# One product of a pair's first unit moved behind the second unit, with the gathering and the sums of pieces in another order

## The chip, the cores and the metric

The kernel runs on one core of one Trainium2 chip. The metric is the device time of one execution in microseconds (us). Five engines work side by side, each through its own instructions in order: PE (matrix products), DVE and ACT (elementwise work), POOL and SP, which here mostly send transfers (DMAs). They wait for one another through semaphores. Sums of products are built in PSUM, which has eight banks; everything else lies in SBUF or in device memory.

## The reference

Let `xn` be x (2048 rows of 448) after a layer norm. The result is x + s * silu(g), with

```
a = xn @ dft_hid_re.T ;  b = xn @ dft_hid_im.T
s = dft_seq_re @ a - dft_seq_im @ b          # 2048 x 2048 matrices
g = (gelu(xn @ w_gate) * (xn @ w_up)) @ w_down
```

The change concerns s alone, in the last stage, from about 491 us on.

## The kernel before, in words

Operands that need more than one pass are held as a high half (rounded, type fp32r) and a low half (the rest). ACT writes the high half and DVE subtracts it to get the low half; the helper `split` does both, at lines L119 (ACT) and L120 (DVE).

The first stages compute the norm, then g by products of gate, up and down, and then a and b for all 16 tiles of 128 rows of the sequence. During the stage of g, sums of matrices of C (the sequence matrices) are made by transfers and kept in device memory (`sums`). silu(g) goes to device memory too (`gv`).

**The last stage.** The rows of the result (index t) are treated in eight pairs of row tiles, j = 0 to 7. For each pair the kernel runs 16 steps, called units, numbered u = 0 to 15 within the pair and m through all pairs. Units 0 to 13 (`u < NS`, NS = 14) each take one sequence tile k and use a scheme of seven products in place of eight: the seven pieces of C for this pair and tile, each 128 x 128, are multiplied with seven pieces of a and b, called T (`TS[k]`, each piece 224 columns in high and low halves, so 448 wide). Each product has its own PSUM bank and sums up over the 14 units. In `seven` (L971) one product is two matmuls: the high half of the C piece by the whole T piece (L977), and the low half by the high half of T (L980). Units 14 and 15 ("t0", "t1") add the two sequence tiles left over by plain products, unit 14 for the first row tile and unit 15 for the second (`plain`, L992 to L994), each in a bank `py`.

**Banks.** Seven products and one plain product make eight banks; unit 15 uses the bank of the first product again. From pair to pair the list of banks turns by one, so that the last of the seven products of the next pair takes the bank in which unit 14 of this pair left its plain product. That product starts only when DVE has read the bank, at L1074.

**Pieces of C.** `load_c` (L870) loads a unit's raw pieces: three from `ct` (L881) and two from `sums` (L882), by SP; for units 14 and 15 one load from `cp` (L879). `sum_c` (L884) forms two more pieces on DVE (L888, L889, 128 x 128 each). `prep_c` (L893) splits all pieces of a unit into high and low halves, in one of four buffers that go round with m, and then loads the raw pieces of the unit five later into the place just freed. At step m the main loop calls `sum_c(m + 4)` and then `prep_c(m + 3)`.

**End of a pair.** `gather` (L996) takes the seven sums out of their banks into the four quarters of the pair's result, two row tiles `cc`: ACT copies the first product (L1000), then seven additions on DVE follow (L1002 to L1008). Three of these run at step 13, the other four at step 14; L1074 adds the plain product of unit 14 at step 15. What is left is put in the list `spare`, of which one entry is taken per step from step 0 of the next pair: for the first row tile add the two halves (L1021) and multiply with silu(g) (L1015) and have POOL add x by an accumulating transfer (L1017); add the second plain product (L1096); the same two for the second row tile. The two finished row tiles are stored by SP (L1019) at steps 5 and 8 (`STORE_AT`).

**Swaps.** Not all T tiles fit into SBUF. Two of them are replaced in each pair, in eight transfers by SP (L1045) at steps 2 to 9. In the last pair, step 12 runs units 12 and 13 together, product by product, and the gathering takes place there.

The order on each engine is the order in which this program calls the operations. There is no planner; only waits for data, for free buffers and for free banks delay an instruction.

Of the kernel before, what the change touches and what calls it, by code (L numbers as in the profile page):

```python
# [13 lines left out]
P = 128  # L14
S = 2048
D = 448
DX = 512
F = 1792
NK = S // P
# [8 lines left out]
HD = D // 2  # L28
# [6 lines left out]
NS = len(KS)  # L35


def order(j):

    return [*KX[j % 2], *KR, *KX[(j + 1) % 2]]  # L40
# [5 lines left out]
def fnet_geglu(ctx: ExitStack, tc: tile.TileContext, x, ca, ct, cp, et, wgu, wd, out):  # L46
# [13 lines left out]
    nc = tc.nc  # L60
# [37 lines left out]
    def bank(i, name):  # L98
        return psum.tile([P, 512], F32, name=name, tag=f"b{i}")
# [18 lines left out]
    def split(h, l, src):  # L118
        nc.scalar.activation(h, src, AF.Copy)  # L119
        nc.vector.tensor_sub(l, src, h)  # L120
# [300 lines left out]
    with tc.manual_schedule():  # L421
# [366 lines left out]
        TS, ab, behind = {}, {}, []  # L788
# [61 lines left out]
        units = [(j, k) for j in range(NK // 2) for k in order(j) + ["t0", "t1"]]  # L850
        UN = NS + 2

        def raw_at(m):
            if m in (4, 5, 9, 10):
                return cc[:, 896 * ((m + 1) % 5) :][:, :896]
            i = (2, 0, 1, 2, 0, 0, 0, 1, 2)[m] if m < 9 else (m - 11) % 5
            return a_r[:, 896 * i :][:, :896] if i < 3 else new["d0"][:, 896 * (i - 3) :][:, :896]
# [4 lines left out]
        def slot_at(m):  # L862
            return (
                lambda: (rest(new["tmp"]), rest(a_x[0])),
                lambda: (unit_at(0), unit_at(1)),
                lambda: (unit_at(2), unit_at(3)),
                lambda: (unit_at(4), rest(a_x[3])),
            )[m % 4]()
# [15 lines left out]
        def sum_c(m):  # L884

            if m < len(units) and not isinstance(units[m][1], str):
                _, cr1, ci1, s2, s1, _, s4 = [raw_at(m)[:, i * P : (i + 1) * P] for i in range(7)]
                nc.vector.tensor_add(s2, cr1, s1)  # L888
                nc.vector.tensor_add(s4, s2, ci1)  # L889

        c_hl = {}

        def prep_c(m):  # L893

            if m >= len(units):
                return
            n = (4 if isinstance(units[m][1], str) else 7) * P
            h, l = [v[:, :n] for v in slot_at(m)]
            split(h, l, raw_at(m)[:, :n])
            c_hl[m] = h, l  # L900
            n = nxt.get(m, m + 5)
            if n:
                load_c(n)

        for k in [*range(14), 15, 14]:
            ps = hid_mm(k)
# [52 lines left out]
        def load_gx(j, t):  # L959
            if 2 * j + t < NK:  # L960
                nc.sync.dma_start(gx[t], gv[:, 2 * j + t])


        LOAD_AT = 2
        STORE_AT = 5, 8
        GX_AT = 11, 12

        PARTS = slice(0, 6, 5), slice(2, 4), slice(4, 7, 2), slice(1, 2)
        PRODUCTS = {1: (1, 0), 6: (3, 5), 2: (2, 2), 7: (5, 3), 5: (4, 4), 3: (6, 6), 4: (0, 1)}

        def seven(m, ps, n=1):  # L971

            for q, (i, b) in PRODUCTS.items():
                for u in range(m, m + n):
                    v = TS[units[u][1]][:, b * D : (b + 1) * D]
                    h, l = [w[:, i * P : (i + 1) * P] for w in c_hl[u]]
                    nc.tensor.matmul(  # L977
                        ps[q][:, :D], h, v, start=u % UN == 0, stop=False, skip_group_check=True
                    )
                    nc.tensor.matmul(  # L980
                        ps[q][:, :HD], l, v[:, :HD],
                        start=False, stop=u % UN == NS - 1, skip_group_check=True,
                    )

        def plain(m, py):
            h, l = c_hl.pop(m)
# [9 lines left out]
        def gather(ps):  # L996

            p = {q: v[:, :D].rearrange("p (w d) -> p w d", w=2) for q, v in ps.items()}
            c11, c12, c21, c22 = [cv[t][:, :, s] for t in range(2) for s in range(2)]
            nc.scalar.activation(c11, p[1], AF.Copy)  # L1000
            return [
                lambda: nc.vector.tensor_sub(c12, c11, p[6]),  # L1002
                lambda: nc.vector.tensor_add(c11, c11, p[2]),
                lambda: nc.vector.tensor_add(c21, c12, p[7]),
                lambda: nc.vector.tensor_sub(c12, c12, p[5]),
                lambda: nc.vector.tensor_sub(c22, p[5], c21),
                lambda: nc.vector.tensor_add(c12, c12, p[3]),
                lambda: nc.vector.tensor_sub(c21, p[4], c21),  # L1008
            ]
# [14 lines left out]
        spare, stores = [], []  # L1024
        for m, (j, k) in enumerate(units):
            u = m % UN
            if u == 0:
                ps = {q: bank(banks[i], f"p{q}_{j}") for i, q in enumerate(PRODUCTS)}
            if u < NS:
                if j < NK // 2 - 1 or u < NS - 2:  # L1030
                    seven(m, ps)
                elif u == NS - 2:

                    seven(m, ps, 2)

                over = 8 if j < NK // 2 - 1 else 7
                for i in range(8):
                    if u != LOAD_AT + i * over // 8:
                        continue
                    i, h = divmod(i, 4)  # L1040
                    TS[KX[(j + 1) % 2][i]] = TS[KX[j % 2][i]]
                    n = KX[(j + 1) % 2][i]
                    a, b = [v.rearrange("p (b d) -> p b d", d=D) for v in (TS[n], td[n])]
                    a, b = a[:, PARTS[h]], b[:, PARTS[h]]
                    nc.sync.dma_start(a.bitcast(F32), b)  # L1045
            else:
                py = bank(banks[7 if u == NS else 0], f"py{u - NS}_{j}")
                plain(m, py)
            if u in GX_AT:
                load_gx(j, GX_AT.index(u))  # L1050

            if u == NS + 1 and m < len(units) - 1:
                todo.pop()()
            if m:
                sum_c(m + 4)
            if u == NS - 2 and j == NK // 2 - 1:
                prep_c(m + 3)
                todo = gather(ps)
                todo.insert(6, lambda: nc.vector.tensor_add(cs[0][0], cs[0][0], cs[0][1]))
                for f in todo:  # L1060
                    f()
            elif u == NS - 1 and j == NK // 2 - 1:
                pass
            elif u == NS - 1:
                todo = gather(ps)
                for f in todo[:3]:
                    f()
                prep_c(m + 3)
            elif u == NS:
                for f in todo[3:] if j < NK // 2 - 1 else ():  # L1070
                    f()
                prep_c(m + 3)
                c = cs[0][0]
                todo = [lambda c=c, py=py: nc.vector.tensor_add(c, c, py[:, :D])]  # L1074
            elif m == len(units) - 1:
                x_ = [raw_at(m + 1 + t)[:, :D] for t in range(2)]
                y = raw_at(m + 3)[:, :D]
                c1, c0 = cs[1][0], cs[0][0]
                nc.vector.tensor_add(c1, c1, cs[1][1])
                todo.pop()()  # L1080
                for c, t in ((c1, 1), (c0, 0)):
                    nc.vector.tensor_mul(c, c, gx[t])
                for c, t in ((c1, 1), (c0, 0)):
                    nc.vector.tensor_add(c, c, x_[t])
                nc.sync.dma_start(ov[:, NK - 2], c0)
                halves = slice(0, HD), slice(HD, D)
                for e in halves:
                    nc.vector.tensor_mul(y[:, e], gx[1][:, e], py[:, e])
                for e, eng in zip(halves, (nc.sync, nc.scalar)):
                    nc.vector.tensor_add(c1[:, e], c1[:, e], y[:, e])  # L1090
                    eng.dma_start(ov[:, NK - 1, e], c1[:, e])
            elif u == NS + 1:
                prep_c(m + 3)
                c = cs[1][0]
                spare = give(j, 0)
                spare.append(lambda c=c, py=py: nc.vector.tensor_add(c, c, py[:, :D]))  # L1096
                spare += give(j, 1)
                banks = banks[1:] + banks[:1]
            else:
                if m:  # L1100
                    prep_c(m + 3)
                if m == 4:
                    sums14()
                if m == 6:
                    hid_split(14)()
                    load_c(14)
                    load_c(15)
                if spare:
                    spare.pop(0)()
                if u in STORE_AT and stores:  # L1110
                    stores.pop(0)()
# [57 lines left out]
```

## Time and profile before

| | |
|---|---|
| median of 3 runs | 786.98 us (786.87 to 787.74) |
| the profiled execution's own time | 787.38 us |
| its span in the trace | 785.5 us |
| PE busy | 775.4 us (99%) |
| DVE busy | 593.6 us (76%) |
| ACT busy | 308.3 us (39%) |
| transfers | 134.37 MB, mean 171 GB/s |
| clock granted to PE | 1.00 |

The trace is of one execution, whose own time is the span and 1.9 us around it. A row of a timeline has the start in us from the start of the span, the duration in us, the engine, the line and the operation, the tile written and the tile read with their shapes, and in square brackets the idle time of the engine ahead of it with what ended it. SPq and POOL rows are the sending of transfers. A row of busy shares has a stretch, its length, the busy time of PE, weight loads, DVE, ACT and POOL with their counts, PE's clock, the busy share of the 16 transfer engines, and GB/s.

### The profile page before, as it was taken

How to read it: one execution, taken by the hardware profiler on the slowest of the kernel's cores; microseconds unless marked ns; L12 is line 12 of the kernel's file. 1: busy time of each engine (PE TensorE's matmuls, PEld its weight loads, DVE VectorE, ACT ScalarE, POOL GpSimd, SP SyncE). 2: the span in 40 equal slices, each digit the busy share in tenths (PEclk: the TensorE clock that was granted, in tenths of full speed). 3: DMA queues.
4: the chain of work that ended last, by engine and by line, in shares of the span. 5: the costliest groups of instructions: out<-in, count | busy, mean ns of one | idle time of the engine just before them, and what ended most of it. 6: DMA issues, size and time to landing. Idle time of an engine off the chain costs nothing.

```text
span 785.5 us, 11220 instructions
## 1 busy us (share of the span) xinstructions
PE 775.4 (99%) x4092; PEld 696.0 (89%) x4092; DVE 593.6 (76%) x1045; ACT 308.3 (39%) x430; POOL 51.6 (7%) x82
## 2 busy tenths in 40 slices
PE   9999999999999999999999999999999999999997
PEld 7888888888888888888889999999999989899997
DVE  7877876767766776776675676888888796969687
ACT  3874432331322322322232864544343444344341
POOL 1000211110110010100000000000000000000000
PEclk9999999999999999999999999999999999999999
DMA  8000575353292360546101651778796969697885
GB/s 317 25 0 28 166 220 117 121 121 117 49 257 54 121 139 6 167 138 145 35 13 58 248 228 51 235 260 278 239 314 212 340 179 348 195 346 215 298 252 191
DMA packets 66103, 134.37 MB, mean 171 GB/s; under 512 B 6784, under 2 KB 53760, under 8 KB 65152
## 3 DMA queue, kind: packets, MB, share of 16 engines
q1 hardware_dynamic: 61008, 109.22, 39.9%
q0 software_dynamic: 4896, 24.32, 14.0%
q8 instruction: 32, 0.52, 0.3%
q14 instruction: 23, 0.19, 0.1%
q10 hardware_dynamic: 144, 0.11, 0.0%
HBM read 119.87 MB, written 43.12 MB: 208 GB/s over the span
## 4 chain that ended last, share of the span: by engine, by line
PE 78%; DMA 11%; DVE 8%; issue 2%; SPq 0%; ACT 0%; DVEq 0%
PE x L346 23%; PE po L326 17%; PE p L977 11%; PE ab L803 9%; PE x L354 5%; PE p L980 5%; PE gu L276 4%; DMA ts_u<-td 2%; DVE w L120 2%; DMA f<-sums 2%; DVE xt L120 2%; DMA out<-cc 2%; DMA raw<-sums 1%; DMA raw<-wgu 1%; DMA raw<-ct 1%
## 5 line engine op out<-in xcount | busy, mean ns | idle before, releaser
L326 PE MATMUL po<-wd,hs 128*128 128x448 f32 x672 | 153.0, 366 | 0.0
L326 PEld LDWEIGHTS po<-wd,hs 128*128 128x128 f32 x672 | 125.8, 188 | 14.3
L346 PE MATMUL x<-xt,w 128*128 128x512 f32 x504 | 135.0, 391 | 0.0
L346 PEld LDWEIGHTS x<-xt,w 128*128 128x128 f32 x504 | 94.6, 188 | 16.9
L335 DVE TENSOR_TENSOR gacc<-gacc,po 128x448 f32<-128x448 f32 x96 | 59.0, 617 | 61.0 <-PE po L326 61.0
L119 ACT ACTIVATE w<-raw 128x896 fp32r<-128x896 f32 (+1 forms) x61 | 55.2, 906 | 71.9 <-DVE raw L889 45.9
L346 PE MATMUL x<-thl,w 128*128 128x512 f32 x288 | 77.5, 391 | 0.3 <-DVE tmp L406 0.3
L803 PE MATMUL ab<-w,xt 128*128 128x448 f32 x256 | 68.0, 365 | 0.0
L346 PEld LDWEIGHTS x<-thl,w 128*128 128x128 f32 x288 | 54.0, 188 | 11.6 <-DVE tmp L406 0.7
L354 PE MATMUL x<-xt,w 128*128 128x512 f32 x192 | 59.2, 390 | 0.0
L977 PE MATMUL p<-xt,w 128*128 128x448 f32 x168 | 54.1, 374 | 0.0
L401 ACT ACTIVATE hs<-tmp 128x512 fp32r<-128x512 f32 x24 | 15.2, 633 | 95.4 <-DVE tmp L399 95.4
L803 PEld LDWEIGHTS ab<-w,xt 128*128 128x128 f32 x256 | 48.1, 188 | 3.8
L386 ACT ACTIVATE tmp<-x 128x512 f32<-128x512 f32 x24 | 14.4, 598 | 90.0 <-PE x L354 90.0
L119 ACT ACTIVATE w<-f 128x896 fp32r<-128x896 f32 (+1 forms) x34 | 30.2, 888 | 48.9 <-DVE f L889 29.6
L120 DVE TENSOR_TENSOR w<-raw,w 128x896 fp32r<-128x896 f32 (+1 forms) x41 | 42.9, 1047 | 3.0 <-ACT w L119 1.3
L354 PEld LDWEIGHTS x<-xt,w 128*128 128x128 f32 x192 | 36.0, 188 | 7.7
L977 PE MATMUL p<-ts_u,ts_tmp 128*128 128x448 f32 x112 | 37.4, 379 | 3.1 <-DVE cc L1074 3.1
L888 DVE TENSOR_TENSOR raw<-raw 128x128 f32<-128x128 f32 x69 | 19.8, 287 | 25.1 <-DMA raw<-sums 25.0
L977 PE MATMUL p<-ts_u,w 128*128 128x448 f32 x112 | 36.4, 374 | 0.0
L977 PE MATMUL p<-hs,w 128*128 128x448 f32 x112 | 35.6, 374 | 0.0
L803 PE MATMUL ab<-wd,xt 128*128 128x448 f32 x96 | 35.1, 365 | 0.0
(234 smaller groups left out, 1599.9 us busy)
## 6 DMA issues: line engine op xcount, KB each, us to landing
ts_u<-td SPq DMA_DIRECT2D x48, 448.0 KB, 6.1
sums<-ca SPq DMA_DIRECT2D x16, 896.0 KB, 7.3
sums<-ca POOLq DMA_DIRECT2D x16, 896.0 KB, 8.8
raw<-ct SPq DMA_DIRECT2D x69, 192.0 KB, 4.4
raw<-sums SPq DMA_DIRECT2D x69, 128.0 KB, 3.7
f<-ct SPq DMA_DIRECT2D x39, 192.0 KB, 3.8
raw<-wgu SPq DMA_DIRECT2D x14, 512.0 KB, 4.3
td<-ts_u POOLq DMA_DIRECT2D x4, 1568.0 KB, 6.6
```

Of the source, the lines that this page charges most:

```text
L119: nc.scalar.activation(h, src, AF.Copy)
L120: nc.vector.tensor_sub(l, src, h)
L276: nc.tensor.matmul(ps[:, cols], a, xt[:, k, cols], start=n == 0, stop=n == len(mm) - 1)
L326: nc.tensor.matmul(po[:, :D], hs[:, a, kk * P : (kk + 1) * P], wdn[:, b, i], start=n == 0, stop=n == 5,)
L335: nc.vector.tensor_add(ga, ga, po[:, :D])
L346: nc.tensor.matmul(ps, a[i], b[j], start=first and n == 0, stop=n == 2, skip_group_check=True)
L354: nc.tensor.matmul(ps, w["k3" + "gu"[g]][0], xt[:, 3], start=False, stop=True, skip_group_check=True)
L401: nc.scalar.activation(hs[:, 0], g1, AF.Copy)
L803: nc.tensor.matmul(p[:, :D], a, b, start=n == 0, stop=n == len(mm) - 1)
L888: nc.vector.tensor_add(s2, cr1, s1)
L977: nc.tensor.matmul(ps[q][:, :D], h, v, start=u % UN == 0, stop=False, skip_group_check=True)
L980: nc.tensor.matmul(ps[q][:, :HD], l, v[:, :HD], start=False, stop=u % UN == NS - 1, skip_group_check=True,)
```

## The change

Four things change, all in the main loop of the last stage. The line numbers behind it move by a few lines (L1074 becomes L1080, L1045 becomes L1049, L1096 becomes L1102).

- In units 0 and 1 of a pair the order of the products is six of unit 0, six of unit 1, then the seventh of unit 0 and the seventh of unit 1.
- At step 13 the split of unit 0 of the next pair comes first, then the copy and four additions of the gathering, then the sums of unit 1, then the other three additions. Before, the sums of unit 1 came first, then the copy and three additions, then the split.
- At step 14 the split of unit 1 comes ahead of the sums of unit 2, and no additions are left. Before, the sums came first, then four additions, then the split.
- Entries of `spare` are taken from step 1 on instead of step 0, and the stores are at steps 6 and 9 instead of 5 and 8.

```diff
--- before.py
+++ after.py
@@ -962,25 +962,25 @@


         LOAD_AT = 2
-        STORE_AT = 5, 8
+        STORE_AT = 6, 9
         GX_AT = 11, 12

         PARTS = slice(0, 6, 5), slice(2, 4), slice(4, 7, 2), slice(1, 2)
         PRODUCTS = {1: (1, 0), 6: (3, 5), 2: (2, 2), 7: (5, 3), 5: (4, 4), 3: (6, 6), 4: (0, 1)}

-        def seven(m, ps, n=1):
-
-            for q, (i, b) in PRODUCTS.items():
-                for u in range(m, m + n):
-                    v = TS[units[u][1]][:, b * D : (b + 1) * D]
-                    h, l = [w[:, i * P : (i + 1) * P] for w in c_hl[u]]
-                    nc.tensor.matmul(
-                        ps[q][:, :D], h, v, start=u % UN == 0, stop=False, skip_group_check=True
-                    )
-                    nc.tensor.matmul(
-                        ps[q][:, :HD], l, v[:, :HD],
-                        start=False, stop=u % UN == NS - 1, skip_group_check=True,
-                    )
+        def seven(ps, *todo):
+
+            for q, m in todo:
+                i, b = PRODUCTS[q]
+                v = TS[units[m][1]][:, b * D : (b + 1) * D]
+                h, l = [w[:, i * P : (i + 1) * P] for w in c_hl[m]]
+                nc.tensor.matmul(
+                    ps[q][:, :D], h, v, start=m % UN == 0, stop=False, skip_group_check=True
+                )
+                nc.tensor.matmul(
+                    ps[q][:, :HD], l, v[:, :HD],
+                    start=False, stop=m % UN == NS - 1, skip_group_check=True,
+                )

         def plain(m, py):
             h, l = c_hl.pop(m)
@@ -1027,11 +1027,15 @@
             if u == 0:
                 ps = {q: bank(banks[i], f"p{q}_{j}") for i, q in enumerate(PRODUCTS)}
             if u < NS:
-                if j < NK // 2 - 1 or u < NS - 2:
-                    seven(m, ps)
+                if u < 2:
+
+                    q, last = list(PRODUCTS)[:6], list(PRODUCTS)[6]
+                    seven(ps, *[(i, m) for i in q], *[(last, i) for i in (m - 1, m) if u])
+                elif j < NK // 2 - 1 or u < NS - 2:
+                    seven(ps, *[(i, m) for i in PRODUCTS])
                 elif u == NS - 2:

-                    seven(m, ps, 2)
+                    seven(ps, *[(i, n) for i in PRODUCTS for n in (m, m + 1)])

                 over = 8 if j < NK // 2 - 1 else 7
                 for i in range(8):
@@ -1051,7 +1055,7 @@

             if u == NS + 1 and m < len(units) - 1:
                 todo.pop()()
-            if m:
+            if m and u not in (NS - 1, NS):
                 sum_c(m + 4)
             if u == NS - 2 and j == NK // 2 - 1:
                 prep_c(m + 3)
@@ -1062,14 +1066,16 @@
             elif u == NS - 1 and j == NK // 2 - 1:
                 pass
             elif u == NS - 1:
+                prep_c(m + 3)
                 todo = gather(ps)
-                for f in todo[:3]:
+                for f in todo[:4]:
                     f()
+                sum_c(m + 4)
+                for f in todo[4:]:
+                    f()
+            elif u == NS:
                 prep_c(m + 3)
-            elif u == NS:
-                for f in todo[3:] if j < NK // 2 - 1 else ():
-                    f()
-                prep_c(m + 3)
+                sum_c(m + 4)
                 c = cs[0][0]
                 todo = [lambda c=c, py=py: nc.vector.tensor_add(c, c, py[:, :D])]
             elif m == len(units) - 1:
@@ -1105,7 +1111,7 @@
                     hid_split(14)()
                     load_c(14)
                     load_c(15)
-                if spare:
+                if u and spare:
                     spare.pop(0)()
                 if u in STORE_AT and stores:
                     stores.pop(0)()
```

## The prediction

> **What bounds the kernel now.** I read the page first, then the waits of PE, then the timelines of PE, DVE and SP at a change of pairs, and last the busy shares of the transfers over one pair.
>
> ```profile
> span 785.5 us, 11220 instructions
> PE 775.4 (99%) x4092; PEld 696.0 (89%) x4092; DVE 593.6 (76%) x1045; ACT 308.3 (39%) x430; POOL 51.6 (7%) x82
> ...
> L977 PE MATMUL p<-ts_u,ts_tmp 128*128 128x448 f32 x112 | 37.4, 379 | 3.1 <-DVE cc L1074 3.1
> ```
>
> PE looks full; in the stage of t its only listed waits are 3.1 us, all on one DVE line, L1074. The change touches nothing ahead of that stage. The timeline of PE, at the change of pairs at 635 us and at the last plain product (L994) ahead of three other changes:
>
> ```profile
> 526.97 0.37 PE L994 MATMUL py<-xt,xt 128*128 128x448 f32 x1
> ...
> 562.55 0.37 PE L994 MATMUL py<-xt,xt 128*128 128x448 f32 x1
> ...
> 635.27 0.37 PE L994 MATMUL py<-xt,xt 128*128 128x448 f32 x1
> ...
> 635.47 0.36 PE L977 MATMUL p<-ts_u,ts_tmp 128*128 128x448 f32 x1
> ...
> 637.24 0.27 PE L980 MATMUL p<-ts_u,xt 128*128 128x224 f32 x1
> ...
> 638.34 0.47 PE L977 MATMUL p<-ts_u,ts_tmp 128*128 128x448 f32 x1 [0.83 <-DVE cc L1074]
> ...
> 744.53 0.37 PE L994 MATMUL py<-xt,xt 128*128 128x448 f32 x1
> ...
> 747.05 0.47 PE L977 MATMUL p<-ts_u,ts_tmp 128*128 128x448 f32 x1 [0.28 <-DVE cc L1074]
> ```
>
> Six products of the first unit run from 635.47, one pair of matmuls each 0.31 us; the seventh would start at 637.34 and starts at 638.34, because its bank still holds the first plain product that L1074 reads. A pair of row tiles without the wait takes 562.55 - 526.97 = 35.58 us. The next five take 744.53 - 562.55 = 181.98, or 36.40 each: 4.1 us are lost in five changes. The sixth lists 0.28; as the listed 0.83 cost 1.0, I take 0.5 for it: 4.6 us in all, an estimate. That is what PE alone could give back.
>
> But why is L1074 late? DVE's rows of the same change, with one of ACT:
>
> ```profile
> 628.74 0.29 DVE L888 TENSOR_TENSOR f<-f 128x128 f32<-128x128 f32 x1 [3.21 <-DMA f<-sums]
> ...
> 629.27 0.68 DVE L120 TENSOR_TENSOR xt<-raw,w 128x512 fp32r<-128x512 f32 x1
> 629.43 0.95 ACT L119 ACTIVATE ts_tmp<-f 128x896 fp32r<-128x896 f32 x1
> ...
> 630.69 0.29 DVE L888 TENSOR_TENSOR f<-f 128x128 f32<-128x128 f32 x1 [0.74 <-DMA f<-sums]
> ...
> 631.23 0.61 DVE L1002 TENSOR_TENSOR cc<-cc,p 128x448 f32<-128x448 f32 x1
> ...
> 631.95 0.62 DVE L1003 TENSOR_TENSOR cc<-cc,p 128x448 f32<-128x448 f32 x1
> ...
> 637.67 0.61 DVE L1074 TENSOR_TENSOR cc<-cc,py 128x448 f32<-128x448 f32 x1
> ...
> 638.73 1.08 DVE L120 TENSOR_TENSOR w<-raw,w 128x896 fp32r<-128x896 f32 x1
> ...
> 641.26 0.62 DVE L1021 TENSOR_TENSOR cc<-cc 128x448 f32<-128x448 f32 x1
> ```
>
> DVE starts when the pieces of the next pair's unit 0 land (628.74; call it E), waits 0.74 for those of unit 1, and then works without a gap past the end of the change. Its work frees the piece buffers; only then does SP send further loads and the first swap of T tiles (L1045). From there the transfers run full until the next E:
>
> ```profile
> 519.73 0.29 DVE L888 TENSOR_TENSOR raw<-raw 128x128 f32<-128x128 f32 x1 [2.50 <-DMA raw<-sums]
> 521.12 0.29 DVE L888 TENSOR_TENSOR raw<-raw 128x128 f32<-128x128 f32 x1 [0.17 <-DMA raw<-sums]
> ...
> 665.21 0.29 DVE L888 TENSOR_TENSOR f<-f 128x128 f32<-128x128 f32 x1 [2.34 <-DMA f<-sums]
> ...
> 737.46 0.29 DVE L888 TENSOR_TENSOR raw<-raw 128x128 f32<-128x128 f32 x1 [2.42 <-DMA raw<-sums]
> ```
> ```profile
> 644.35 1.74 SPq L1045 DMA_DIRECT2D ts_u<-td  x1
> ```
> ```profile
> 527.17:539.00 11.83, 11.83 (x77) 11.27 (x76) 11.62 (x25) 4.78 (x5) 0.92 (x1) 1.00 0.59 160
> 539.00:555.86 16.86, 16.86 (x109) 16.10 (x108) 11.01 (x21) 7.00 (x8) 0.90 (x1) 1.00 1.05 365
> ...
> 645.00:649.00 4.00, 4.00 (x28) 3.81 (x27) 3.93 (x9) 1.78 (x3) 0.22 (x1) 1.00 0.92 224
> ```
>
> (The last two columns are the share of the transfer engines and GB/s.) So a loop without PE sets the pace: E at 628.74, swap issued at 644.35 (15.6 us of DVE and SP), next E at 665.21 (20.9 us of transfers). Its mean period is (737.46 - 519.73)/6 = 36.29 us against PE's own 35.58. PE waits because the loop is slower; removing the wait alone moves nothing beyond a one-time slack.
>
> **The change part by part.** *The seventh product moves behind six of unit 1.* Same matmuls, no cost on PE. Its bank is now needed six products (1.9 us) later, at 635.47 + 12 x 0.31 = 639.2. Late next could be unit 1's low half, needed at 637.3, and unit 2's, needed at 639.85. Unit 0's piece buffer is read until about 639.6 instead of 638.9, so the split of unit 4 may start only then; DVE reaches it later still, so I cost it at nothing.
>
> *DVE's order.* In starts of instructions, from the rows above: sums of one unit 0.53, a low half (L120, 896 wide) 1.0, L1002 0.72, each other gathering step 0.53. New order: ACT's split of unit 0 now goes before the gathering copy L1000 and ends at 629.43 + 0.95 = 630.38; DVE does unit 0's low half 630.4, L1002 631.4, L1003 to L1005 to 633.7, sums of unit 1 to 634.25, L1006 to L1008 to 635.85, unit 1's low half (done 636.9, 0.4 ahead of need), sums of unit 2 636.85, the old L1074 at 637.4 (done 638.0, 1.2 ahead), sums of unit 3, unit 2's low half at 638.45 (done 639.5, 0.3 ahead). No PE wait is left here. Against 638.73 DVE gains 0.3; a wait of 0.45 for ACT has replaced one of 0.74 for a transfer. I take 0.2, since the second wait differs between changes; at the first one, 521.12 - 519.73 is only 1.39 instead of 1.95, and DVE loses 0.35.
>
> *The pieces of work kept for later* (`spare`: L1021 and the steps behind it) start at step 1 instead of 0. By 641.26 one step of 0.53 has run ahead of unit 4's low half; now none has. Loads and swaps go out 0.2 + 0.53 = 0.73 earlier, measured from E.
>
> *What of it the transfers pass on.* The POOL accumulation that `spare` issues, at 644.35 beside the first swap, goes out some 0.9 later:
>
> ```profile
> 644.35 0.87 POOL L1017 DMA_DIRECT2D cc<-x  x1 [29.60 <-DVE f L888]
> ```
>
> Its 224 KB at 365 GB/s are 0.6 us that may be pushed from the stretch with free capacity (share 0.92) into the full one. Bounds: 0 to 0.6 lost; I take 0.2, nearer the free end, because the loads in the 0.92 stretch nearly fill it anyway. Net per loop: 0.73 - 0.2 = 0.53. Period 35.76, still above PE's 35.58. The first loop gives -0.35 + 0.53 - 0.2 = 0, the six after it (the last one to the end) 6 x 0.53 = 3.2 us.
>
> *The stores go one step later*, behind a swap and a pair of loads. They stand in the same queue, the loads behind them gain, so within a pair I cost the shift at nothing if they land before L1004 overwrites their tile. For the pair at 665: sent at 662.9 (behind the second row below), needed at E + 4.0 = 669.2, 6.3 us later; landing took 5.7 in the median.
>
> ```profile
> 660.22 0.38 SPq L1019 DMA_DIRECT2D out<-cc  x1
> ...
> 662.56 0.32 SPq L882 DMA_DIRECT2D raw<-sums  x1
> ```
> ```profile
> DMA to landing us min/median/max: 5.3/5.7/7.4
> ```
>
> *The tail.* The last pair's gathering starts behind ACT's split of the last load of C (L119 at 772.05 below), which was sent at 765.77 and landed 6.2 later, at 771.97. The row names PE, which ends at the same moment; I take the transfer, the queue being full until then, so the tail moves with the loop. There the second store moves behind the load of x, which itself waits for DVE until 769.46:
>
> ```profile
> 765.77 0.33 SPq L879 DMA_DIRECT2D raw<-cp  x1
> ...
> 767.87 0.38 SPq L1019 DMA_DIRECT2D out<-cc  x1
> 769.46 0.33 SPq L875 DMA_DIRECT2D f<-x  x1
> ```
> ```profile
> DMA to landing us min/median/max: 6.2/6.2/6.2
> ```
> ```profile
> 772.05 0.63 ACT L119 ACTIVATE w<-raw 128x512 fp32r<-128x512 f32 x1 [1.22 <-PE p L977]
> ```
> ```profile
> 774.58 0.61 DVE L1004 TENSOR_TENSOR cc<-cc,p 128x448 f32<-128x448 f32 x1
> ...
> 781.42 0.67 DVE L1088 TENSOR_TENSOR f<-ts_g,py 128x224 f32<-128x224 f32 x2
> ```
> ```profile
> 780.65 0.36 PE L994 MATMUL py<-xt,xt 128*128 128x448 f32 x1
> ```
>
> Sent at 769.85, it lands at 775.15 (5.3) to 777.25 (7.4) on this clock; L1004 wants its tile at 774.58. From L1004 to L1088 DVE is full and starts L1088 0.4 us after PE is done (781.0), so a delay there reaches the end. Bounds 0.5 to 2.6; the queue empties here, so I take 0.5.
>
> **Sum.** -3.2 + 0.5 = -2.7 us. The profiled execution took 787.38 (span 785.5), so 784.7; the median, 786.98, stands 0.4 below it, so 784.3.
>
> **The rivals.** (1) PE alone: nothing new is late, the loop shortens to PE's pace and the tail goes with PE; all 4.6 us come back: 782.4. For it: the margins above are positive, and nothing of the 0.73 need be lost. Against it: the forecast period, 35.76, and the store in the tail; so it has the smaller chance. The Trainium skill, Perfetto Trace Analysis, Optimization Strategy, says to find the gaps of the busiest engine and make what blocks it start or finish sooner; taken by itself that rule gives this rival's sum, and the periods of 36.29 and 35.58 do not bear it out, as the blocker is itself paced by transfers.
>
> (2) The transfers pass nothing on: the full stretch grows by what it gains at its start (0.73). E keeps its period, PE waits elsewhere (at a low half), and the tail's 0.5 is paid: 787.5. For it: share 1.05 over 16.9 us; against it: the stretch holds the same bytes and would start earlier.
>
> (3) Slower: the store lands too late for L1004 in each pair. From 6.3 us after its issue L1004 waits with all of DVE behind it; from 6.3 + 0.53 = 6.8 the loop is slower than before. At the largest landing shown, 7.4, a pair loses 1.1 - 0.53 = 0.57; six times, with the tail, 3.9 us: 790.9. Against it: 5.7 in the median. The Trainium skill, DMA: Bandwidth & Descriptors, Rules for kernel authors, speaks against this edit: issue a transfer early and wait for it late. By that rule the shorter distance must cost; these rows say only beyond 6.3 us.
>
> (4) The change does not do what it says: unit 1's products come ahead of their low half and PE waits there as long as before. The margin of 0.4 and 0.3 us speaks against it; it would end like (2).
>
> **How the numbers follow.** Forecast 0.50 (its own range 783.2 to 785.4), (1) 0.23, (2) with (4) 0.12, (3) 0.15. About 0.2% (1.6 us) is what a measurement of this kernel can tell from no change. Of the forecast 0.03 falls within it, as do (2) and (4): faster 0.70, same 0.15, slower 0.15. The range goes from just under (1) to (2): 782.2 to 787.6.
>
> **What would show it.** Right: no PE wait on the old L1074; the first L888 of successive pairs 35.6 to 35.9 us apart; the first swap some 0.7 us sooner after E; L1004 of the last pair idle for about 0.5 us. Wrong: periods of 36.3 (transfers pass nothing on) or 35.58 with a larger gain; PE waits on L120 at unit 1 or 2; DVE waits at L1004 inside pairs.

## The result and the profile after

The changed kernel takes 789.6 us in the median (787.49 to 790.45), the kernel before in the same comparison 786.87 us (785.95 to 787.74). The ratio is 1.0032, with a 95% interval of 1.0021 to 1.0044: slower by some 2.5 us. The forecast was 784.3 us and its range ended at 787.6, so both sign and size were wrong. The profiled execution after took 790.45 us, 3.07 above the one before; its span is 788.5, 3.0 above. It is the slowest of its eight runs, 0.85 above their median, so what its loop shows is somewhat too bad.

The page of the kernel after, and below it the waits of PE in the last stage (the columns: total us, times, longest):

```profile
span 788.5 us, 11189 instructions
...
PE 777.4 (99%) x4092; PEld 695.0 (88%) x4092; DVE 594.5 (75%) x1045; ACT 307.9 (39%) x430; POOL 51.6 (7%) x82
...
L977 PE MATMUL p<-ts_u,ts_tmp 128*128 128x448 f32 x112 | 37.4, 376 | 0.0
```
```profile
PE p L980 <- DVE w L120: 1.1, 5, 0.3
PE p L977 <- DMA ts_u<-td: 0.3, 1, 0.3
```

The wait on the addition of the first plain product (L1074 before, L1080 now) is gone, as forecast, and PE waits less by this list: 1.4 us instead of 3.1. Yet the kernel is slower. Its waits have moved to the low halves of units 1 and 2 and to a swapped T tile.

The loop that the prediction called the pace-maker shows why. DVE's timeline at the first, second, third and last change of pairs after the change:

```profile
518.93 0.29 DVE L888 TENSOR_TENSOR raw<-raw 128x128 f32<-128x128 f32 x1 [2.15 <-DMA raw<-sums]
...
556.19 0.29 DVE L888 TENSOR_TENSOR raw<-raw 128x128 f32<-128x128 f32 x1 [2.69 <-DMA raw<-sums]
...
557.95 1.09 DVE L120 TENSOR_TENSOR xt<-raw,ts_tmp 128x896 fp32r<-128x896 f32 x1 [0.54 <-ACT ts_tmp L119]
558.96 0.61 DVE L1002 TENSOR_TENSOR cc<-cc,p 128x448 f32<-128x448 f32 x1
...
560.22 0.61 DVE L1004 TENSOR_TENSOR cc<-cc,p 128x448 f32<-128x448 f32 x1
560.93 0.62 DVE L1005 TENSOR_TENSOR cc<-cc,p 128x448 f32<-128x448 f32 x1
...
563.60 1.08 DVE L120 TENSOR_TENSOR w<-raw,w 128x896 fp32r<-128x896 f32 x1
...
565.13 0.61 DVE L1080 TENSOR_TENSOR cc<-cc,py 128x448 f32<-128x448 f32 x1
...
566.64 1.09 DVE L120 TENSOR_TENSOR w<-f,w 128x896 fp32r<-128x896 f32 x1 [0.36 <-ACT w L119]
...
593.34 0.29 DVE L888 TENSOR_TENSOR raw<-raw 128x128 f32<-128x128 f32 x1 [2.51 <-DMA raw<-sums]
...
739.34 0.29 DVE L888 TENSOR_TENSOR raw<-raw 128x128 f32<-128x128 f32 x1 [2.99 <-DMA raw<-sums]
```

E, the first L888 of the next pair's unit 0, now comes every (739.34 - 518.93)/6 = 36.74 us, against 36.29 before; 35.76 was forecast. Between E and unit 2's low half (the last L120 of these rows) DVE no longer waits for unit 1's pieces (0.74 before). Instead it waits 0.54 for ACT's split of unit 0, loses 0.2 between L1004 and L1005 (0.71 from start to start; 0.53 had been reckoned), and waits 0.36 for ACT's split of unit 2. At the changes near 593, 630 and 702 us this last wait is 0.17 and isn't listed. There unit 2's low half starts at E + 10.17; before it was E + 9.99, and E + 9.71 was forecast. The rows that send the first swap and the first accumulating transfer in the same change:

```profile
571.73 0.38 SPq L1049 DMA_DIRECT2D ts_u<-td  x1
...
573.79 0.38 SPq L1049 DMA_DIRECT2D ts_u<-td  x1
```
```profile
573.82 0.87 POOL L1017 DMA_DIRECT2D cc<-x  x1 [30.11 <-DVE f L888]
```

The swap goes out at E + 15.54, and in the mean of changes 2 to 6 at E + 15.31 against 15.63 before: 0.32 sooner, not 0.73. The accumulation goes out with the second swap, at E + 17.63 here and E + 17.3 in other changes, 1.7 later than before (15.6). And the stretch from the first swap to the next E, which is bound by transfers, has become longer: 21.32 us against 20.69. So in these loops 0.3 us are gained at the start and 0.6 lost behind it. The first loop, which was forecast to come out even, loses 1.13: there the swap goes out at E + 15.36 instead of 15.04, and the stretch behind it takes 21.90 instead of 21.09.

The last rows of the span, from DVE's and ACT's timelines:

```profile
777.63 0.62 DVE L1004 TENSOR_TENSOR cc<-cc,p 128x448 f32<-128x448 f32 x1 [0.70 <-DMA out<-cc]
```
```profile
774.31 0.63 ACT L119 ACTIVATE w<-raw 128x512 fp32r<-128x512 f32 x1 [1.79 <-DMA raw<-cp]
```

From the last E to the end it takes 49.2 us instead of 48.0; 0.70 of that is the wait for the store, and the row of ACT names the load of C that the prediction took for the tail's releaser. The account of the span: E starts 0.8 sooner, six periods of 0.45 more give 2.7, the tail 1.1: together 3.0.

### The profile page after: what moved, and what is told of

It is laid out like the page before. It is cut to its first block, busy times and chain, and to the rows that moved or that the text cites. A ratio compares the mean times of both kernels' runs of the same rounds, so it can differ in the third digit from the quotient of the medians.

```text
span 788.5 us, 11189 instructions
## 1 busy us (share of the span) xinstructions
PE 777.4 (99%) x4092; PEld 695.0 (88%) x4092; DVE 594.5 (75%) x1045; ACT 307.9 (39%) x430; POOL 51.6 (7%) x82
## 4 chain that ended last, share of the span: by engine, by line
PE 71%; DMA 17%; DVE 8%; issue 2%; ACT 1%; SPq 1%; DVEq 0%; ACTq 0%
PE x L346 23%; PE po L326 17%; PE ab L803 9%; PE p L977 7%; PE x L354 5%; DMA raw<-ct 5%; PE gu L276 4%; PE p L980 4%; DMA ts_u<-td 3%; DMA f<-sums 2%; DMA f<-ct 2%; DVE w L120 2%; DVE xt L120 2%; DMA raw<-sums 2%; DMA raw<-wgu 1%
## 5 line engine op out<-in xcount | busy, mean ns | idle before, releaser
L120 DVE TENSOR_TENSOR w<-raw,w 128x896 fp32r<-128x896 f32 (+1 forms) x41 | 42.9, 1048 | 2.7 <-ACT w L119 1.8
L888 DVE TENSOR_TENSOR raw<-raw 128x128 f32<-128x128 f32 x69 | 19.8, 288 | 22.1 <-DMA raw<-sums 22.1
```

## The experiments

Each kernel was timed side by side with the kernel before, and the ratio compares these two. The four parts of the change are called product order, gathering order (steps 13 and 14), late pieces of work (`spare` from step 1) and later stores (steps 6 and 9). The table holds the results; "swap" is the mean time from E to the first swap in changes 2 to 6, "stretch" the mean from there to the next E, both from the profiled execution.

| kernel | ratio to before (95%) | median us | period | swap | stretch |
|---|---|---|---|---|---|
| before (timed with after) | | 786.87 | 36.29 | 15.63 | 20.69 |
| after | 1.0032 (1.0021 to 1.0044) | 789.6 | 36.74 | 15.31 | 21.32 |
| product order alone | 1.0002 (.9992 to 1.0012) | 786.24 | 36.24 | 15.68 | 20.50 |
| gathering order alone | 1.0024 (1.0015 to 1.0033) | 788.24 | 36.34 | 15.90 | 20.41 |
| product + gathering order | 1.0022 (1.0013 to 1.0032) | 787.91 | 36.24 | 15.84 | 20.39 |
| late work + later stores | .9975 (.9963 to .9988) | 784.59 | 35.90 | 14.54 | 21.27 |
| late work alone | 1.000 (.999 to 1.001) | 786.89 | 36.11 | 15.12 | 21.04 |
| later stores alone | .9965 (.9953 to .9978) | 783.58 | 35.59 | 15.10 | 20.44 |
| all but the gathering order | .9976 (.9966 to .9985) | 784.67 | 35.81 | 14.56 | 21.24 |
| product order + later stores | .9965 (.9952 to .9978) | 783.86 | 35.92 | 15.13 | 20.91 |
| gathering order + later stores | 1.0029 (1.0017 to 1.004) | 789.28 | 36.57 | 15.84 | 20.71 |
| later stores, first accumulation late | 1.0013 (.9999 to 1.0027) | 788.23 | 36.25 | 15.08 | 21.17 |
| before, no accumulation | .9946 (.9934 to .9958) | 782.64 | 35.34 | 16.23 | 19.15 |
| after, no accumulation | .9946 (.9934 to .9958) | 782.61 | 35.68 | 16.26 | 19.50 |
| gathering + stores, sums of unit 2 first | 1.0011 (1.0003 to 1.0019) | 787.55 | 36.31 | 15.70 | 20.51 |
| gathering + stores, gathering first | .9975 (.9967 to .9984) | 784.56 | 35.71 | 15.26 | 20.35 |

A profile is one execution and its loop numbers scatter: product order alone has a stretch 0.19 under that of the kernel before at the same time in the runs. For such differences only the ratio decides.

**The product order alone.** The kernel before with the new order of products in units 0 and 1.

```diff
-                if j < NK // 2 - 1 or u < NS - 2:
+                if u < 2:
+                    q, last = list(PRODUCTS)[:6], list(PRODUCTS)[6]
+                    seven(ps, *[(i, m) for i in q], *[(last, i) for i in (m - 1, m) if u])
+                elif j < NK // 2 - 1 or u < NS - 2:
```

> The kernel before with the product order alone changed (six of unit 0, six of unit 1, then both sevenths). Three theories of where the changed kernel loses its 2.7 us: A, late accumulations (spare from step 1 sends the two accumulating transfers some 2 us later, into the full stretch, which grows by 0.9 us); B, the order of gathering and splitting delays DVE and ACT; C, the later stores. All three say that this edit alone leaves the pace, since the loop from one E to the next does not hold PE: periods of E 36.2 to 36.4 us, time 786 to 787.3; the wait on the read of the plain product goes and PE waits instead for a low half of unit 1 or 2. A theory in which PE sets the pace gives 782.5 to 784.

The ratio is 1.0002: nothing. Its waits of PE:

```profile
PE p L980 <- DVE w L120: 0.6, 3, 0.2
```

The 3.1 us on L1074 have become 0.6 at low halves, and by the ratio the time stays: its interval, 0.9992 to 1.0012, has no room for the 4.6 us (0.6%) that PE alone could give back. So PE's wait was a consequence of the loop and not its cause. (The profiled execution, 785.82, is near the lowest of its runs, so its waits and its period are a little too good.)

**The gathering order alone, and with the product order.** The kernel before with steps 13 and 14 of after; then both orders.

```diff
+                prep_c(m + 3)
                 todo = gather(ps)
-                for f in todo[:3]:
+                for f in todo[:4]:
                     f()
-                prep_c(m + 3)
+                sum_c(m + 4)
+                for f in todo[4:]:
+                    f()
```

> The kernel before with the order of gathering, splitting and sums at steps 13 and 14 alone changed. A: no loss, 786 to 787.5, first swap at E + 15.7 to 15.9 (the changed kernel's 15.25 and the piece of spare work, 0.53, ahead of it again), stretch from swap to next E 20.5 to 20.8. B: the whole loss lies here, 789 or more, with ACT's split of unit 2 late. C: as A.

> The changed kernel with spare work from step 0 and stores at 5 and 8 again, so products and gathering changed, the rest as before. A: 786 to 787.5, stretch 20.5 to 20.8, swap at E + 15.8, period 36.3 to 36.6. B: 789 to 790, as the changed kernel. C: as A.

The gathering order alone is slower, 1.0024, and the first swap goes out 0.27 later after E. With the product order it is the same, 1.0022. (The profiled execution of the latter, 786.6, is the lowest of its runs, so its loop numbers are too good.) The prediction had this part as a gain of 0.2 per change. None of the three theories in these expectations holds alone: 788.24 for the gathering order lies above the range of A and C and below that of B.

**Late pieces of work and later stores, together and apart.**

```diff
-        STORE_AT = 5, 8
+        STORE_AT = 6, 9
...
-                if spare:
+                if u and spare:
```

> The kernel before with spare work from step 1 and stores at steps 6 and 9 alone. A: the stretch from first swap to next E grows from 20.6 to 21.4 or more, accumulations at E + 17.5, but the swap goes out 0.5 sooner, so the period is 36.5 to 36.8 and the time 788 to 790. B: the swap goes out 0.5 sooner and nothing is lost, 784 to 786. C: as A, told apart later.

> The kernel before with spare work from step 1 alone (stores at 5 and 8 as before). Theory F, two opposite effects: the later stores let the pieces of unit 1 land sooner (the wait of 0.74 goes), the later spare work sends the swap 0.53 sooner but the accumulations 1 us later, which lengthens the stretch of transfers by 0.8. F here: the wait of 0.7 stays, swap at E + 15.1, accumulations at E + 17.1, stretch 21.4, period 36.5, time 786.5 to 788. Rival G, the stretch grew because of the stores' place in SP's queue: stretch 20.6, period 35.7, time 783 to 784.5.

> The kernel before with stores at 6 and 9 alone (spare work from step 0). F: the wait for unit 1's pieces goes, swap at E + 15.1, accumulations as much sooner, stretch 20.6, period 35.7, time 782.5 to 784.5. G: stretch 21.4, period 36.5, time 786.5 to 788.

Together they are faster, .9975, where theory A expected 788 to 790 us. Apart, the late work is worth nothing (1.000): the swap goes out 0.51 sooner and the stretch behind it is 0.35 longer. The later stores alone are, with the kernel that adds the product order to them, the fastest in this study that compute everything, .9965 or 783.6 us; the prediction had costed them at nothing within a pair. DVE's timeline of that kernel at the change near 627 us, with the first swap in SP's:

```profile
626.88 0.29 DVE L888 TENSOR_TENSOR f<-f 128x128 f32<-128x128 f32 x1 [2.67 <-DMA f<-sums]
...
628.29 0.29 DVE L888 TENSOR_TENSOR f<-f 128x128 f32<-128x128 f32 x1 [0.19 <-DMA f<-sums]
...
634.27 1.08 DVE L120 TENSOR_TENSOR w<-f,w 128x896 fp32r<-128x896 f32 x1
635.27 0.61 DVE L1074 TENSOR_TENSOR cc<-cc,py 128x448 f32<-128x448 f32 x1
...
636.33 1.08 DVE L120 TENSOR_TENSOR w<-raw,w 128x896 fp32r<-128x896 f32 x1
```
```profile
641.96 0.38 SPq L1045 DMA_DIRECT2D ts_u<-td  x1
```

The second L888 waits 0.19 for unit 1's pieces instead of 0.74: with the store one step later these pieces land sooner after those of unit 0. SP's rows show why. They hold the second load of unit 0, the second load of unit 1 and the second store of the pair; the kernel before, whose store (660.22) and load of unit 1 (662.56) the prediction shows, has

```profile
659.69 0.43 SPq L882 DMA_DIRECT2D f<-sums  x1
```

and with the later stores it is

```profile
655.64 0.42 SPq L882 DMA_DIRECT2D f<-sums  x1
...
657.85 0.32 SPq L882 DMA_DIRECT2D raw<-sums  x1
...
659.03 0.34 SPq L1019 DMA_DIRECT2D out<-cc  x1
```

Before, the store stood between the loads of the two units, and unit 1's went out 2.87 after unit 0's; now it stands behind both, and they are 2.21 apart. At every change but the first, ahead of which no store is sent, the wait is 0.7 to 0.9 in the kernel before, with the product order alone and with the late work alone, and below 0.3 in each kernel that has the later stores and the old gathering order. The swap follows at E + 15.08. PE has no wait listed in the whole stage, the loop's period is 35.59, and PE's own is 35.58: the loop has come down to PE's own pace, and this without any of the other edits. Which of the two stores does it was not run apart; the order in the queue points to the second.

**Everything but the gathering order, and the product order with later stores.**

> The kernel before with the product order and the later spare work and stores, without the order of gathering. F: pace as with the later work alone (36.0), PE's remaining waits of 0.4 gone, 783.5 to 785. If the product order costs something beside the later work: 785.5 or more.

> The kernel before with the product order and the later stores alone. F: loop 35.7, no wait on the read of the plain product, 781.5 to 784, the fastest of all. G: 786 to 788.

.9976 and .9965: beside the later stores, too, the product order is worth nothing, and the late work may cost about 0.1% (.9975 and .9976 against .9965; the intervals overlap).

**The gathering order with the later stores.**

> The kernel before with stores at 6 and 9 and the new order of gathering alone. Theory B1, the new order gives away what the later stores bring, because DVE now waits for ACT where it waited for unit 1's pieces: swap at E + 15.8, period 36.3, time 787 to 789. Rival, the two effects add up: swap at 15.4, time 784.5 to 786.

It is slower than before, 1.0029. Its DVE rows at the same change:

```profile
629.93 0.29 DVE L888 TENSOR_TENSOR f<-f 128x128 f32<-128x128 f32 x1 [3.09 <-DMA f<-sums]
...
631.69 1.09 DVE L120 TENSOR_TENSOR xt<-f,ts_tmp 128x896 fp32r<-128x896 f32 x1 [0.54 <-ACT ts_tmp L119]
...
633.96 0.61 DVE L1004 TENSOR_TENSOR cc<-cc,p 128x448 f32<-128x448 f32 x1
634.68 0.62 DVE L1005 TENSOR_TENSOR cc<-cc,p 128x448 f32<-128x448 f32 x1
...
637.34 1.08 DVE L120 TENSOR_TENSOR w<-f,w 128x896 fp32r<-128x896 f32 x1
638.34 0.28 DVE L888 TENSOR_TENSOR raw<-raw 128x128 f32<-128x128 f32 x1
...
640.09 1.09 DVE L120 TENSOR_TENSOR w<-raw,w 128x896 fp32r<-128x896 f32 x1
```
```profile
PE p L977 <- DVE cc L1076: 4.7, 6, 1.1
```

Unit 2's low half starts at E + 10.16 here and at E + 9.45 with the later stores alone: 0.71 later. The terms: a wait of 0.54 in place of 0.19 (0.35), 0.18 more from L1004 to L1005, and the last 0.17 ahead of unit 2's low half (L888 at 638.34, the old L1074 and the sums of unit 3 take 1.58 and it starts 1.75 later). The swap goes out 0.74 later in the mean, and the ratio is 0.64% worse. PE, with the old order of products, again waits for the old L1074 (here L1076), 4.7 us in six changes, as the loop is late again. So the gathering order throws away more than the later stores had won: with unit 1's pieces there in time, the old order has only 0.19 of waiting left that a new one could replace.

**Which piece of the gathering order.** The kernel just shown, once with the sums of unit 2 ahead of the split of unit 1 at step 14, as before, and once with the copy and three additions ahead of the split of unit 0 at step 13, as before.

```diff
             elif u == NS:
-                prep_c(m + 3)
                 sum_c(m + 4)
+                prep_c(m + 3)
```

> New gathering order and later stores, but at step 14 the sums of unit 2 go ahead of the split of unit 1, as in the kernel before. Theory A (the price of the new order is DVE's wait of 0.54 us for ACT's split of unit 0 at step 13, with the 0.2 us gap behind L1004): only the wait of 0.17 us for unit 2's split goes; first swap 15.6 to 15.8 us after E, ratio 1.001 to 1.003. Theory B (the price is the sums of unit 2 standing behind the split of unit 1, which make ACT late): first swap back at 15.1 us, ratio about .997.

```diff
             elif u == NS - 1:
-                prep_c(m + 3)
                 todo = gather(ps)
-                for f in todo[:4]:
+                for f in todo[:3]:
                     f()
+                prep_c(m + 3)
+                todo[3]()
```

> New gathering order and later stores, but at step 13 the copy and three additions go ahead of the split of unit 0, as in the kernel before. Theory A (the price of the new order is DVE's wait of 0.54 us for ACT's split of unit 0): that wait is gone, first swap 15.1 to 15.4 us after E, ratio .9965 to .999, about 784 to 786 us. Theory B (the price is the sums of unit 2 behind the split of unit 1): first swap stays at 15.8 us, ratio about 1.003.

The first goes from 1.0029 to 1.0011, with the swap 0.14 sooner; the second to .9975, with the swap 0.58 sooner. Theory A holds: most of the price is at step 13. In the second kernel DVE works through the first additions while ACT splits, and at this change no wait behind E is listed:

```profile
627.97 0.69 DVE L120 TENSOR_TENSOR xt<-raw,w 128x512 fp32r<-128x512 f32 x1
628.57 0.62 DVE L1002 TENSOR_TENSOR cc<-cc,p 128x448 f32<-128x448 f32 x1
...
630.36 1.08 DVE L120 TENSOR_TENSOR xt<-f,ts_tmp 128x896 fp32r<-128x896 f32 x1
631.36 0.61 DVE L1005 TENSOR_TENSOR cc<-cc,p 128x448 f32<-128x448 f32 x1
```

L1005 also follows at once there, 0.2 of the price: a split stands between it and L1004. The rows have 0.72 from start to start in two places, from L1002 to L1003 and from L1004 to L1005 when nothing is between; in both the second addition writes the quarter of the result that the first one reads. The other additions of the gathering that follow one another are 0.53 or 0.54 apart. That the overlap is the reason was not tested.

**The accumulating transfers.** First both kernels without them (in the first seven pairs x isn't added to the result):

```diff
-                nc.gpsimd.dma_start(c, xv[:, 2 * j + t, :D], accum_op=ALU.add)
```

> The kernel before without the accumulating transfers (x is not added to the first seven pairs of row tiles). A1: the stretch is some 1.5 to 3 us shorter, the pace is PE's, 782 to 784. To be compared with the changed kernel without them.

> The changed kernel without the accumulating transfers (x is not added to the first seven pairs of row tiles). A1: the stretch is as long as in the kernel before without them, so that the pair differs by the earlier swap and the tail alone: time from 1.5 us less to 1 us more than that kernel. H: it is still 2 us or more slower.

Both have the ratio .9946 and take 782.6 us: without the accumulations the two kernels are equal, some 4 us below the one before, and the stretch falls by 1.5 to 1.8 us. So the accumulations are part of what sets the pace. That the two kernels are equal says less: both then have about PE's own pace (35.34 and 35.68), and a difference in the loop could no longer show. Then the later stores, with only the first accumulation one step later (the second plain product is added ahead of it):

```diff
-                spare.append(lambda c=c, py=py: nc.vector.tensor_add(c, c, py[:, :D]))
+                spare.insert(1, lambda c=c, py=py: nc.vector.tensor_add(c, c, py[:, :D]))
```

> The kernel before with stores at 6 and 9, and in the spare work the second plain product's addition ahead of the first row tile's multiplication, so that only the first accumulation goes out one step (2.1 us) later; DVE does the same work in each step. Theory A1, the late accumulation lengthens the stretch of transfers: swap at E + 15.1 as with the later stores alone, stretch 20.8 to 21.3 instead of 20.4, period 35.9 to 36.4, time 785 to 787. Rival H, the stretch grows because it starts earlier and its end is held by something else: stretch 20.4, time 783.6.

1.0013 against .9965: 2.07 us later for one transfer per pair costs nearly 0.5% of the whole. The swap is where it was (15.08), the stretch grows by 0.73. Busy shares of both kernels at the same change, first the stretch from swap to E, then E + 16 to 18, 18 to 20 and 20 to 22 (the last two columns are the share of the transfer engines and GB/s). Later stores alone:

```profile
641.96:661.78 19.82, 19.82 (x129) 18.92 (x128) 15.25 (x29) 8.91 (x10) 1.74 (x2) 1.00 1.02 333
642.88:644.88 2.00, 2.00 (x15) 1.92 (x14) 1.97 (x5) 0.89 (x2) 0.00 (x0) 1.00 0.78 135
644.88:646.88 2.00, 2.00 (x14) 1.91 (x14) 1.97 (x5) 0.89 (x2) 0.00 (x0) 1.00 1.05 257
646.88:648.88 2.00, 2.00 (x14) 1.90 (x14) 1.97 (x5) 0.89 (x2) 0.73 (x1) 1.00 1.06 395
```

With the first accumulation late:

```profile
642.96:664.68 21.72, 21.72 (x141) 20.74 (x140) 15.16 (x29) 9.39 (x11) 1.74 (x2) 1.00 0.97 317
643.88:645.88 2.00, 2.00 (x15) 1.91 (x14) 1.97 (x5) 0.89 (x2) 0.86 (x1) 1.00 0.83 206
645.88:647.88 2.00, 2.00 (x15) 1.92 (x14) 1.97 (x5) 0.89 (x2) 0.01 (x1) 1.00 0.67 224
647.88:649.88 2.00, 2.00 (x14) 1.90 (x14) 1.97 (x5) 0.89 (x2) 0.73 (x1) 1.00 0.81 195
```

At this change, with the accumulation early, all transfers together are at 395 GB/s from E + 20 on; with it late they move 195 to 224 GB/s at shares of .67 to .83 until E + 22. Beside the second accumulation (E + 21.3) there is no such drop: with the later stores alone the three windows of 2 us from E + 22 on have 388, 341 and 314 GB/s. What the transfer engines wait for, the rows don't say. But one thing the profile shows: the account of the queues for the stretch from the swap to E, in which all transfers of POOL's queue (q0) are these two accumulations (packets, MB, and the time of the packets as a share of what 16 engines have), first in the kernel before, then with the first accumulation late:

```profile
q0 software_dynamic: 288, 0.46, 13.9%
```
```profile
q0 software_dynamic: 288, 0.46, 11.9%
```

Of 20.86 and 21.72 us that is 1.45 and 1.29 us of all 16 engines for each accumulation, twice or more the 0.6 that its bytes come to at 365 GB/s. It does not grow when the transfer goes late. It stays open whether the lateness costs or that the two accumulations now lie 4.1 instead of 6.2 us apart; the late work alone moves both by 1.55 and keeps them 6.2 apart, and there the stretch grows by 0.35.

**The parts together.** By ratios: later stores -0.35%, the gathering order beside them +0.64%, late work +0.10%, the product order 0: +0.39%, or 3.1 us, against 0.32% measured, within the intervals.

## Why the prediction was wrong

- *What bounds the kernel* was right. PE's waits on L1074 followed from the loop of DVE, SP and transfers; without them (product order alone) nothing changes. That is also why rival (1), PE alone, did not come by this edit. The Trainium skill, Perfetto Trace Analysis, Optimization Strategy, looks for what blocks the busiest engine; here the blocker named by the wait was taken away and the ratio was 1.0002, while a shorter loop (later stores) removed PE's listed waits altogether without touching that edge.
- *The seventh product moves* at no cost: right.
- *DVE's order* is the step that failed first, and it set the sign: with everything but this order the kernel is faster (.9976), with it slower (1.0032). The prediction gave it a gain of 0.2 per change; alone it lost 0.27, beside the later stores 0.74. At 556 us unit 0's low half started at E + 1.76, 0.1 behind the forecast, as the wait for ACT is 0.54 and not 0.45. From L1004 to L1005 it took 0.71 and not 0.53; the tail of the profile before shows the same distance when the two follow each other (774.58, quoted in the prediction, to 775.30). And unit 2's low half was forecast without any wait, because ACT's own order at step 14 was not followed: with the sums of unit 2 behind the split of unit 1, ACT can begin on unit 2 only when they are formed, and DVE waits 0.36 there and 0.17 at other changes. Above all the comparison was with a wait of 0.74 that another part of the same change takes away.
- *The pieces of work kept for later*: 0.53 sooner forecast, 0.51 measured in the swap. Right.
- *What of it the transfers pass on* failed second. The accumulation was said to go out 0.9 later; a whole step (2.07, from swap to swap) less the 0.5 by which the steps come sooner makes 1.55, and 1.55 was measured with the late work alone, 1.7 in after. Its price was bounded at 0 to 0.6 by its own bytes and taken as 0.2; in after the stretch grew by 0.63, with the late work alone by 0.35, and with one accumulation late by 0.73, beyond the bound. The bytes were the wrong measure: in the trace of the kernel before the packets of one accumulation take 1.45 us of the 16 engines. How much of that the other transfers pay, the runs show (0.35 to 0.73), but not by which mechanism.
- *The stores go one step later*, costed at nothing within a pair: wrong to the good side. They are worth -0.35%. The prediction said itself that the loads behind the stores gain, and had DVE's wait of 0.74 for these loads in its rows, but gave the gain no size; it is 0.55 per change. L1004 does not wait in any pair but the last, so rival (3), whose 790.9 us lies nearest to the result, is not what happened. The Trainium skill, DMA: Bandwidth & Descriptors, Rules for kernel authors, says to issue a transfer early and wait for it late. For the stores, for which nothing waits within a pair, the runs show the reverse (.9965 when later), as the loads gain by it, and for the accumulations they agree with it (1.0013 when one is later).
- *The tail*: 0.5 forecast for L1004's wait, 0.70 measured. Right in place, a little short. The tail as a whole grew by 1.1.
- *Rival (4)* had the right place: PE waits at the low halves of units 1 and 2 (1.1 us). Its margin of 0.4 and 0.3 went with the two failed terms of DVE's order. But it was priced to keep the old period, and the period grew by 0.45.

## What to carry to other kernels

When the engine that looks full waits for a loop of other engines, measure the loop: the period of one fixed event, and its pieces. Reorder work on an engine only with the partner's order written out beside it, since an instruction moved ahead of its partner's result turns cover into a wait; and measure the parts of a change apart, since here one line (the stores) won 0.35% and another lost more than that. An accumulating transfer was here better kept out of the stretch of full transfers than moved into it, and its price was not given by its bytes; the account of the queues, with the time that the packets take, comes nearer.

## What the hardware showed that was not expected

One accumulating transfer of 224 KB per pair, 2.07 us later, lengthens the stretch behind it by 0.73 us, more than the 0.6 us that its bytes would take at 365 GB/s; its packets take 1.3 to 1.45 us of the 16 engines, late or early. At the change that was looked at, all transfers together moved some 200 GB/s from E + 18 to E + 22, where 257 and then 395 were reached with it early. Without the fourteen accumulations the stretch is 19.15 instead of 20.69 us. And a store that is sent one step later, in the same queue and of the same size, and so behind a load instead of ahead of it, makes this load land 0.5 us sooner after its neighbour and the kernel 0.35% faster.
